# Backward pass of an S4 layer plus a gated FFN on one core: the stores of the decay exponentials go from ScalarE's DMA queue to SyncE's

## The chip, the cores and the metric

The kernel runs on one core of a Trainium2 chip. The time is device microseconds (us) of the whole program. The kernel before took 1819.65 us, the median of three runs (1815.38 to 1821.79).

## The reference, cut to what matters

A layer norm of `x` (2048 tokens, 576 channels) feeds an S4 convolution and a gated FFN; the reference returns the output and the gradients of everything in it but `B_x`.

```python
xn = _layernorm(x)
# A: S4
logdA = exp(log_dt)[:, None] * (A_re + 1j * A_im)          # 576 x 128
P = jnp.exp(logdA[:, :, None] * l[None, None, :])          # decay and phase at 2048 steps
K = jnp.einsum("dn,dnl,dn->dl", Cc, P, dB).real            # then y = causal convolution of xn with K by FFT
# B: FFN
gate = relu(xn @ W_gate); up = xn @ W_up                   # 576 -> 4608
out = x + (y + xn * Dskip) + (gate * up) @ W_down
_out, _vjp = jax.vjp(_f, ...); _grads = _vjp(grad_out)     # 13 outputs
```

## The kernel before, in words

**Two programs in one.** `Ffn.gen` and `S4.gen` are generators that emit instructions and yield an estimate of their TensorE time. The main loop runs `Ffn.gen` and, from the fourth layer-norm group on, lets `S4.gen` catch up to 0.9 of it (`PACE`). So TensorE carries FFN matmuls with small S4 matmuls strewn between them. The FFN loops over 12 chunks `c` of 384 hidden columns, and in each over 4 groups `sg` of 512 tokens:

- `a_unit` (L230): three products of 512 columns (gate, up, and the incoming gradient through `W_down`; L244), whose PSUM banks are read by ScalarE (`rg`, L252; `dhb`, L260) and VectorE (`upm`, L254), and then `hT`, `dgT`, `duT` on VectorE (L256 to L264).
- `t_steps` (L267): these three are turned by TensorE (L273) and copied into `hN`, `dgN`, `duN`.
- `outdx` (L277): the products back to 576 columns (L301), copied to `osx`, added up in DRAM by GpSimd's DMA queue (L312, L314).
- `dw_down`, `dw_gu`, `dw_left` (L330 to L378): the weight gradients of a chunk (L339, L355, L373), copied to `obd` and `obw` and stored by SyncE. They need the four token groups of the chunk, and run in the chunk after it. Their other operand, `rows`, is loaded by SyncE (L326) into four buffers.

All FFN products and turns take their PSUM banks from one rotation of five (`psum_mm`, L1146); S4 has three (`psum_s4`, L1147). `Balance.copy` (L56) gives each copy out of PSUM to VectorE (L62) or ScalarE (L68).

**S4 beside it.** In chunk 1, `S4.gen` runs `p1` (forward transforms of `xn` and the gradient: `fwd1`, L628 with stores of `A_ug`, L632; then `mix`, L645, which reads them back as `b_ug`, L707, writes `s_ug`, stores it, L722; `product`, L666 to L674, into `pr_z`; `unmix`, L655, into `fC`, stored at L728) and `params`, woven together by `both`. `params` holds what the change touches.

**The decay exponentials.** For each of 36 groups of 16 channels, `ex_step` (L582) takes a buffer `exs` of 128 x 640 fp32 from a pool of five (L568), multiplies on VectorE (L585), takes the exponential on ScalarE in place (L586), and stores 320 KB to `ex_dram` (L587). A buffer comes free when its store has landed, so `exs` number n+5 on VectorE waits for store number n. `p2` loads them again later (L817). In this text exs, Exp and store are numbered 1 to 36.

**What sets the order.** Every engine works its own list in order, and a DMA is issued by the engine in whose list it stands: an issue that waits holds up all behind it in that list. The lists are fixed when the program is built, and a scheduler moves instructions past one another there. SyncE (SP) does little else than issue transfers. The transfers of SP and ScalarE (ACT) share eight completion semaphores in turn: in the built lists each issue waits for the transfer that stands eight places before it.

Of the kernel before, what the change touches and what calls it, by code (L numbers as in the profile page):

```python
# [475 lines left out]
class S4:  # L476
# [85 lines left out]
    def params(self, pw):  # L562

        g, nc, bal = self.g, self.g.nc, self.g.bal
        v = nc.vector
        with ExitStack() as c:
            pool = self.pool(c, "par_raw", 1)
            exp_ = self.pool(c, "par_ex", 5)  # L568
            raw = pool.tile([P, 6, D], BF16, name="raw")
            nc.sync.dma_start(raw[:], self.par_in[:])  # L570
            ldt = pool.tile([P, D], BF16, name="ldt")
            nc.sync.dma_start(ldt[:], self.log_dt.rearrange("(o d) -> o d", o=1).to_broadcast([P, D]))
            yield 1.0
            dt = pool.tile([P, D], F32, name="dtf")
            nc.scalar.activation(dt[:], ldt[:], ACT.Exp)
            nc.sync.dma_start(self.dt_dram[:], dt[:])
            Ar, Ai, Br, Bi, Cr, Ci = (raw[:, i, :] for i in range(6))
            v.tensor_tensor(pw[:, 0, :], Ar, dt[:], op=ALU.mult)
            bal.add(d=0.7, a=0.7)
            yield 1.0  # L580

            def ex_step(i):  # L582
                shp = [P, SX, NE]
                ex = exp_.tile(shp, F32, name="exs")
                v.tensor_tensor(ex[:], pw[:, 0, i * SX:(i + 1) * SX].unsqueeze(2).to_broadcast(shp), self.ev[:].unsqueeze(1).to_broadcast(shp), op=ALU.mult)  # L585
                nc.scalar.activation(ex[:], ex[:], ACT.Exp)  # L586
                nc.scalar.dma_start(self.ex_dram[:, i], ex[:])  # L587
                bal.add(d=0.75, a=0.65)

            for i in range(0, 8):  # L590
                ex_step(i)
                yield 1.0
            p1 = pool.tile([P, D], F32, name="p1")
            p2 = pool.tile([P, D], F32, name="p2")
            v.scalar_tensor_tensor(pw[:, 1, :], Ai, 1.0 / TWO_PI, dt[:], op0=ALU.mult, op1=ALU.mult)
            for j, (y1, y2, op) in enumerate(((Br, Bi, ALU.subtract), (Bi, Br, ALU.add))):
                v.tensor_tensor(p1[:], Cr, y1, op=ALU.mult)
                v.tensor_tensor(p2[:], Ci, y2, op=ALU.mult)
                v.tensor_tensor(p1[:], p1[:], p2[:], op=op)
                v.tensor_tensor(pw[:, 2 + j, :], p1[:], dt[:], op=ALU.mult)  # L600
                bal.add(d=2.6)
                yield 2.0
            for i in range(8, D // SX):
                ex_step(i)
                yield 1.0
# [645 lines left out]
```

## Time and profile before

The profiled execution took 1815.38 us, the fastest of the three runs; its span, from the first to the last instruction, is 1813.7 us.

| | before |
|---|---|
| median of 3 runs | 1819.65 us |
| profiled execution, its span | 1815.38 us, 1813.7 us |
| busy: PE, DVE, ACT, POOL | 95%, 75%, 65%, 11% |
| mean granted TensorE clock | 0.993 |
| 36 `exs` multiplications (VectorE) | 825 ns each, started at 99.7 to 211.2 us |
| 36 Exp (ScalarE) | 737 ns each |
| 36 store issues (ScalarE's queue) | 326 ns each, at 102.1 to 231.7 us |
| store, issue to landing | 2.2 / 5.3 / 8.1 us (least, median, most) |

PE is TensorE, DVE VectorE, ACT ScalarE, POOL GpSimd, SP SyncE. "Idle before" an instruction is the time its engine waited, and the arrow names what ended the wait; `ACTq` and `SPq` rows are DMA issues. Durations of instructions that follow one another overlap a little, so starts are the better measure of pace (exs run back to back start 0.74 us apart, Exp 0.65 us).

### The profile page before, as it was taken

How to read it: one execution, taken by the hardware profiler on the slowest of the kernel's cores; microseconds unless marked ns; L12 is line 12 of the kernel's file. 1: busy time of each engine (PE TensorE's matmuls, PEld its weight loads, DVE VectorE, ACT ScalarE, POOL GpSimd, SP SyncE). 2: the span in 40 equal slices, each digit the busy share in tenths (PEclk: the TensorE clock that was granted, in tenths of full speed). 3: DMA queues.
4: the chain of work that ended last, by engine and by line, in shares of the span. 5: the costliest groups of instructions: out<-in, count | busy, mean ns of one | idle time of the engine just before them, and what ended most of it. 6: DMA issues, size and time to landing. Idle time of an engine off the chain costs nothing. (4 is left out here: it accounts for less than half of the span.)

```text
span 1813.7 us, 42172 instructions
## 1 busy us (share of the span) xinstructions
PE 1716.0 (95%) x16303; PEld 1184.1 (65%) x16449; DVE 1359.6 (75%) x3181; ACT 1182.3 (65%) x2710; POOL 205.2 (11%) x246
## 2 busy tenths in 40 slices
PE   7978998999999999999999999999899999999998
PEld 5655556668566666766756766766676775676776
DVE  7565886677889788679787889989979963983551
ACT  5865774687588478568468658748756845864551
POOL 0200012012012012011101101101111100110000
PEclk9989999999999999999999999999999999999999
DMA  9789899678558676777857856856666578995873
GB/s 300 264 313 339 267 246 291 181 194 229 179 130 208 176 193 133 223 196 154 219 159 179 233 165 141 218 180 152 170 175 150 94 213 276 256 279 153 265 244 96
DMA packets 239006, 373.32 MB, mean 206 GB/s; under 512 B 49490, under 2 KB 153428, under 8 KB 237268
## 3 DMA queue, kind: packets, MB, share of 16 engines
q1 hardware_dynamic: 207652, 292.29, 50.1%
q0 software_dynamic: 24384, 51.92, 18.9%
q10 hardware_dynamic: 6768, 26.40, 3.9%
q8 instruction: 129, 2.11, 0.5%
q14 instruction: 73, 0.60, 0.1%
HBM read 233.10 MB, written 137.43 MB: 204 GB/s over the span
## 5 line engine op out<-in xcount | busy, mean ns | idle before, releaser
L68 ACT CAST osx<-ps_mm 128x288 bf16<-128x288 f32 x675 | 255.4, 429 | 65.0 <-PE ps_mm L301 61.3
L314 POOL DMA_DIRECT2D acc_dram<-osx x160 | 138.7, 867 | 1058.8 <-ACT osx L68 645.3
L301 PE MATMUL ps_mm<-wf,dgT 128*128 128x288 bf16 x1152 | 207.2, 288 | 5.3 <-DVE upm L254 2.0
L355 PEld LDWEIGHTS <-rows 128*128 128x128 bf16 x1536 | 145.7, 98 | 94.7 <-issue 3.6
L301 PE MATMUL ps_mm<-wf,duT 128*128 128x288 bf16 x1152 | 207.2, 288 | 0.0
L301 PE MATMUL ps_mm<-wf,hT 128*128 128x288 bf16 x1152 | 183.3, 288 | 19.0 <-DVE hT L256 12.7
L244 PE MATMUL ps_mm<-xT,wd_156 128*128 128x512 bf16 x712 | 179.1, 379 | 0.4
L244 PE MATMUL ps_mm<-gT,wd_157 128*128 128x512 bf16 x693 | 175.7, 379 | 2.6 <-DMA gT<-in_gT_dram 2.0
L254 DVE SCALAR_TENSOR_TENSOR upm<-rg,ps_mm 128x512 bf16<-128x512 bf16 x144 | 98.5, 684 | 102.1 <-PE ps_mm L244 72.3
L244 PE MATMUL ps_mm<-xT,wd_155 128*128 128x512 bf16 x595 | 163.5, 379 | 11.3 <-ACT xT L153 1.6
L339 PE MATMUL ps_mm<-rows,hN 128*128 128x144 bf16 x2304 | 158.6, 226 | 0.0
L339 PEld LDWEIGHTS <-hN 128*128 128x128 bf16 x2304 | 147.5, 98 | 3.4 <-issue 0.8
L68 ACT CAST obw<-ps_mm 128x384 bf16<-128x384 f32 x104 | 49.5, 477 | 142.1 <-PE ps_mm L355 113.1
L301 PEld LDWEIGHTS <-hT 128*128 128x128 bf16 x1152 | 104.6, 98 | 50.6 <-DVE hT L256 16.9
L355 PE MATMUL ps_mm<-dgN,rows 128*128 128x384 bf16 x768 | 135.9, 326 | 1.0 <-ACT obw L68 1.0
L355 PE MATMUL ps_mm<-duN,rows 128*128 128x384 bf16 x768 | 136.6, 326 | 0.0
L301 PEld LDWEIGHTS <-duT 128*128 128x128 bf16 x1152 | 113.1, 98 | 31.1 <-issue 1.3
L301 PEld LDWEIGHTS <-dgT 128*128 128x128 bf16 x1152 | 107.7, 98 | 33.0 <-issue 8.0
L252 ACT ACTIVATE rg<-ps_mm 128x512 bf16<-128x512 f32 x144 | 87.2, 606 | 58.7 <-PE ps_mm L244 54.9
L932 DVE TENSOR_REDUCE Sm<-pr 128x8 f32<-128x256 f32 x288 | 120.0, 417 | 3.8
L68 ACT CAST dhb<-ps_mm 128x512 bf16<-128x512 f32 x141 | 83.8, 594 | 53.8 <-PE ps_mm L244 49.9
L244 PEld LDWEIGHTS <-wd_155 128*128 128x128 bf16 x720 | 66.2, 97 | 64.8 <-issue 6.2
(2517 smaller groups left out, 3517.5 us busy)
## 6 DMA issues: line engine op xcount, KB each, us to landing
acc_dram<-osx POOLq DMA_DIRECT2D x176, 288.0 KB, 4.9
gT<-in_gT_dram SPq DMA_DIRECT2D x48, 640.0 KB, 6.2
xT<-xT_dram SPq DMA_DIRECT2D x44, 640.0 KB, 6.2
rows<-in_gq_dram SPq DMA_DIRECT2D x48, 576.0 KB, 4.0
wf<-in_Wf_dram ACTq DMA_DIRECT2D x11, 1296.0 KB, 8.9
ex_dram<-exs ACTq DMA_DIRECT2D x36, 320.0 KB, 5.3
ex<-ex_dram SPq DMA_DIRECT2D x36, 320.0 KB, 4.1
out_dram<-obw SPq DMA_DIRECT2D x96, 96.0 KB, 2.8
```

The source lines that it names most:

```text
L68: self.nc.scalar.copy(out, in_)
L244: nc.tensor.matmul(ps[:], lhsT=w[:, k, fs], rhs=rhs[:, k, :], start=(k == 0), stop=(k == NK - 1))
L252: nc.scalar.activation(rg[:], ps_g[:], ACT.Relu)
L254: nc.vector.scalar_tensor_tensor(upm[:], rg[:], 0.0, ps_u[:], op0=ALU.is_gt, op1=ALU.mult)
L301: nc.tensor.matmul(ps[:, cs], lhsT=lt, rhs=rh, start=(i == 0), stop=(i == len(mms) - 1))
L314: nc.gpsimd.dma_start(g.acc_dram[:, t, :, :], o[:], accum_op=ALU.add)
L339: nc.tensor.matmul(ps[:, ft * 144:(ft + 1) * 144], lhsT=self.hN[:, st, ft * P:(ft + 1) * P], rhs=gq[:, st, :], start=(st == 0), stop=(st = ...
L355: nc.tensor.matmul(ps[:, :Fc], lhsT=xs[:, st, 0:P], rhs=src[:, st, :], start=(st == 0), stop=(st == ST - 1))
L932: nc.vector.tensor_reduce(out=Sm[:, vi, s0 + dd:s0 + dd + DG, :], in_=pr[:], op=ALU.add, axis=AX.X)
```

## The change

One line: the 36 stores are issued by SyncE.

```diff
@@ ex_step
                 nc.scalar.activation(ex[:], ex[:], ACT.Exp)
-                nc.scalar.dma_start(self.ex_dram[:, i], ex[:])
+                nc.sync.dma_start(self.ex_dram[:, i], ex[:])
                 bal.add(d=0.75, a=0.65)
```

The change has been described as "FFN products and FFN turns share one rotation of five PSUM banks instead of three and two"; both kernels have that rotation, and the diff holds nothing of it.

Because the scheduler places the instructions, the built lists differ in more than this line, from about the first exs to the first groups of `p2`; ahead of and behind that stretch they are the same. The number of instructions does not change. SP's list about the first stores, as built (before on the left):

```
L696 sig<-xn                          L696 sig<-xn
L697 sig<-grad_out                    L587 stores 1 to 6
L187 wd_157                           L697 sig<-grad_out
L187 wd_156                           L632 A_ug<-fA_1669
L632 A_ug<-fA_1669                    L587 store 7
L202 xT, L196 gT (token group 1)      L187 wd_157, wd_156
L611, L696, L697                      L632 A_ug<-fA_1699
```

And about the turn from `fwd1` to `mix`, where the old list has the same loads and no store of exs:

```
L632 A_ug (the last), L326 rows, L587 store 10
L707 b_ug x4, L345 obd, L326 rows, L360 obw
L587 stores 11, 12   L326 rows   L360 obw
L587 stores 13, 14   L360 obw
L587 stores 15, 16, 17   L360 obw
L587 stores 18 to 21   L722 s_ug   L707 b_ug   L360 obw   L587 store 22
```

On PE, seven transform matmuls (L628) stand ahead of the first L301 on the new `hT` of chunk 0's last group, where they stood 34 to 56 matmuls behind it. On DVE, one exs (the sixth) stands ahead of `upm` there, not behind it. On ACT, the first five Exp stand together with no issue between them.

## Prediction

> **What bounds the kernel now.** I first read the busy shares and the slices of the page, then busy time by stretch, then who waited for whom on PE, then the timelines of DVE, ACT and SP.
>
> ```profile
> PE 1716.0 (95%) x16303; PEld 1184.1 (65%) x16449; DVE 1359.6 (75%) x3181; ACT 1182.3 (65%) x2710; POOL 205.2 (11%) x246
> ...
> PE   7978998999999999999999999999899999999998
> ```
>
> PE is the bound: outside 98 us it works. So an edit can shorten the time only where PE stands still. Slices are 45.3 us; the third (digit 7) and fourth (8) hold the exs. By stretch (columns: length, PE, PEld, DVE, ACT, POOL busy, clock, DMA share, GB/s):
>
> ```profile
> 100.00:135.00 35.00, 22.99 (x219) 18.02 (x217) 23.89 (x44) 20.54 (x50) 2.31 (x5) 0.85 0.93 334
> 135.00:150.00 15.00, 14.95 (x153) 11.41 (x152) 5.09 (x10) 8.98 (x21) 0.00 (x0) 1.00 1.03 395
> 150.00:190.00 40.00, 34.04 (x220) 17.54 (x222) 25.45 (x54) 22.91 (x49) 0.00 (x0) 1.00 0.96 319
> 190.00:210.00 20.00, 17.25 (x141) 10.43 (x141) 16.94 (x48) 16.16 (x40) 1.75 (x2) 1.00 0.90 263
> 210.00:235.00 25.00, 24.20 (x187) 14.23 (x189) 19.80 (x57) 20.82 (x53) 3.38 (x4) 1.00 0.91 267
> ```
>
> PE idles 12.0 + 0.05 + 6.0 + 2.75 + 0.8 = 21.6 us there: all that the change can win or, so far as it makes such waits, add to. PE's waits from 90 to 240 us:
>
> ```profile
> PE ps_mm L301 <- DVE hT L256: 7.4, 1, 7.4
> PE ps_s_1748 L628 <- DVE fA_1669 L62: 2.7, 1, 2.7
> PE ps_mm L301 <- DVE upm L254: 2.6, 1, 2.6
> PE ps_s_2492 L645 <- ACT s_ug L68: 2.3, 1, 2.3
> PE ps_s_2520 L645 <- DVE s_ug L62: 1.9, 1, 1.9
> PE ps_s_1794 L628 <- DVE fA_1760 L62: 1.6, 1, 1.6
> ```
>
> The first two are one stall from 101.5 to 111.94. Why hT was late, DVE tells:
>
> ```profile
> 104.42 0.69 DVE L254 SCALAR_TENSOR_TENSOR upm<-rg,ps_mm 128x512 bf16<-128x512 bf16 x1
> 109.08 0.82 DVE L585 TENSOR_TENSOR exs<-pw,ev 128x640 f32<-128x640 f32 x1 [3.98 <-DMA ex_dram<-exs]
> 110.72 0.82 DVE L585 TENSOR_TENSOR exs<-pw,ev 128x640 f32<-128x640 f32 x1 [0.82 <-ACT exs L586]
> 111.47 0.42 DVE L256 TENSOR_TENSOR hT<-rg,upm 128x512 bf16<-128x512 bf16 x1
> ```
>
> The sixth and seventh exs stand ahead of hT and wait for buffers, that is for stores 1 and 2. These were issued at 102.14 and 102.8 on ACT and landed at about 109.05 and 110.7, by the exs that waited: 6.9 and 7.9 us, beside wd_157 and wd_156 (480 KB each, issued by SP at 101.83 and 102.36). The second cluster of stalls is at 160 to 170 us, and there ACT was held by its own issues:
>
> ```profile
> 159.62 1.77 ACTq L587 DMA_DIRECT2D ex_dram<-exs  x2
> 161.49 0.74 ACT L586 ACTIVATE exs<-exs 128x640 f32<-128x640 f32 x1 [5.84 <-DMA out_dram<-obw]
> 162.13 0.46 ACT L68 CAST obw<-ps_mm 128x384 bf16<-128x384 f32 x1
> ```
>
> An issue on ACT waited for an SP store (obw), as the eight shared semaphores demand, and the copies of obw and s_ug behind it freed PE's banks late.
>
> **Part 1, what is the same.** PSUM: line 1146 has the five banks already, 0 us. The number of bytes, exs and Exp is the same.
>
> **Part 2, issues from ACT to SP.** ACT loses 36 x 0.326 = 11.7 us of issues and its waits for semaphores (0.49, 3.24, 1.52, 1.34, 5.84 us: 12.4 in all). ACT is 65% busy, so that alone is worth nothing; it counts where PE waits, below. SP gets 36 x 0.33 = 12 us of issues in a stretch of 130 us where it had 92 issues to make. The price is that SP's loads stand behind stores that wait for their Exp.
>
> **Part 3, the stall at 101 us.** In the new list stores 1 to 6 go before the wd loads. DMA was nearly idle from 103.2 to 104.4 us (slices of 110, 23 and 58 GB/s), and A_ug, dt and sig, issued before them, are landing by then. Store 1 can be issued at 102.2. Its landing lies between 2.2 and 8.1 us, the least and most of the 36; I take 2.8, near the least, since nothing large is queued before it. It lands at 105.0, store 2 at about 105.8. Then DVE: exs 6 at 105.0, upm 105.8, exs 7 at 106.4, hT 107.2 to 107.6. On ACT five Exp without issues end near 104.9; the copies that the seven moved L628 need end near 107.8. PE goes on at 108.0 instead of 111.94: 3.9 us. The seven L628 (0.12 us each by starts) are done within the stall: 0.85. Of the 1.6 us wait at 119.88 for fA_1760, which now comes early, I count 0.25, as DVE is full from 113 to 127 us. Sum **5.0 us**. Between the ends: with 2.2, ACT's copies hold PE at 107.8 all the same (+0.2); with 8.1, hT comes at 112.7 and 0.75 of the 5.0 turns to nothing or a small loss.
>
> At half clock PE spent 112 to 115 us (granted 0.50 from 106 to 114, 0.82 to 116). It had fallen within 5 us of the gap's start (1.00 at 102 to 104, 0.62 at 104 to 106); the gap left is some 6 us, so I count nothing for the clock.
>
> **Part 4, 112 to 150 us.** PE is full, and the lead of 5 us is carried if operands are there: wd issued near 109.5, used 139; rows wait for PE's own release and move with it. 0 us.
>
> **Part 5, 146 to 174 us.** Here the new list is a chain. Store 11 stands on SP behind four b_ug loads, which wait for the last A_ug store (151.3 us before, 146.3 with the lead). Four b_ug issues (2.6 us, as before) and three more: store 11 issued 150.5. I call x its landing time and take 5.0: the median of the ACT stores in 150 to 190 us, where SP's own S_ug stores (288 KB) take 5.1:
>
> ```profile
> ex_dram<-exs ACTq DMA_DIRECT2D x16, 320.0 KB, 5.0
> b_ug<-A_ug_184 SPq DMA_DIRECT2D x8, 288.0 KB, 5.3
> ...
> S_ug_186<-s_ug SPq DMA_DIRECT2D x4, 288.0 KB, 5.1
> ```
>
> Landed 155.5; exs 16 (0.75), Exp 16 (0.7), then the third obw copy: 157.4. SP stores it and issues store 16 at 158.3; landed 163.3; exs 20 and 21 end 164.5, Exp 21 165.1, s_ug copy, PE's ps_2492 at 165.6 (before 166.44). Store 21 issued 165.2, landed 170.2; exs 26 ends near 171.9 behind what DVE does, pr_z 172.5, PE's L655 at 172.6 (before 174.4). The lead has shrunk from 5.0 to **1.7**. Three landings are in this chain: lead = 1.7 - 3 (x - 5.0), at most 5.
>
> A rule of the Trainium skill speaks against the change: DMA: Bandwidth & Descriptors, section "Queues, rings and completion order", says that each DMA engine goes round between the queue rows it has work for, so that on ACT's row a store shares the engines with SP's backlog, and on SP's row it stands behind it. By it x would grow. The rows above show no such advantage here (5.0 against 5.1). If the rule ruled, x would go toward the 8.1 of the most, and the sum below toward a loss of 4.7 instead of a gain of 4.6.
>
> **Part 6, 174 to 235 us.** Fewer exs stand on DVE between 177 and 190 us (none, where before there were four, one with a wait of 2.56), so dskip and upm come early and PE's 2.6 us wait at 198 goes: +2.6. Near 200 us exs 34 waits for store 29, which waits for an Exp late in ACT's list: DVE loses about 2 us, as it did before at 211 (2.04 us, after which PE waited 0.65); I count +0.3. The last store comes near 217, not 231.7; p2's loads keep their place.
>
> **Sum:** 1.7 + 2.6 + 0.3 = **4.6 us earlier**; 1815.38 becomes 1810.8. The median stands 4.3 us above the profiled run, so I give 1819.65 - 4.6 = **1815 us**. From p2's first groups on the lists are the same again, and what PE gains it keeps.
>
> **Rivals.** *A, slower:* stores land late on SP. The chain of part 5 decides: the gain is 4.6 - 3 (x - 5.0), nothing at x = 6.5, a loss of 4.7 at 8.1; if the 2.6 of part 6 are lost too, 7.3: 1824 to 1827. For it: SP's rows loads took 6.3 to 9.6 us and its A_ug stores up to 9.5 in 112 to 150 us, with DMA at 1.03. Against it: 5.1 from 150 on. *B, no change:* DMA is full from 130 to 170 us (share 0.92 to 1.04); the lead of part 3 then meets transfers that cannot come sooner, and 0 to 2 us remain: 1818. *C, more:* ACT is free of issues, so copies come sooner and x is 3.5 (the median of ACT's stores in 190 to 235 us); the lead stays 5, and 5 + 2.6 + 0.3 = 8 are won, 11 if half of the 6.0 us from 150 to 190 goes too: 1809 to 1812. *D:* that the diff doesn't do what it says is so for the PSUM words; it is in the sum as 0.
>
> **How the numbers follow.** Forecast (1 to 7 us faster) 0.36; A 0.28; B 0.20; C 0.16. A measurement can tell 0.3% (5.4 us) here. Faster by that: C, and a third of the forecast: 0.27. Slower: two thirds of A (0.19), and 0.06 for what no row shows: 0.25. Same: 0.48. The range goes from C's end, 1819.65 - 11, to A's end with a margin: **1808.5 to 1827.5**; the likeliest case alone has 1812.5 to 1818.5.
>
> **What would show it.** Part 3: stores 1 and 2 land within 4 us, hT at 107 to 108 us, PE idle 100 to 135 us near 7 instead of 12. Part 5: landing times of L587 between 145 and 170 (5 or 8), and PE's L655 (ps_2571) before or after 174.4. Part 6: no PE wait for upm near 198. Wrong if SP's loads (b_ug, xT, gT) come late behind a store and PE waits for a DMA, or if a new wait appears after 240 us.

## The result, and the profile after

The changed kernel takes 1807.84 us (median of four runs, 1805.36 to 1809.66) beside 1820.37 us of the kernel before (four runs): a ratio of 0.9935, with an interval of 0.9912 to 0.9958. A second measurement gave 0.9946 (0.9928 to 0.9964). The change is 10 to 12 us faster. The forecast had the side right, at 1815 us; the time lies just under the low end of its range (1808.5).

The profiled run of after took 1809.66 us, the slowest of its four, with a span of 1808.0; the profiled run of before was the fastest of its own. The two spans differ by only 5.7 us, so the difference has to be read stage by stage, not from the spans. The busy shares and PE's slices:

```profile
PE 1719.4 (95%) x16303; PEld 1185.2 (66%) x16449; DVE 1359.3 (75%) x3181; ACT 1181.1 (65%) x2710; POOL 205.0 (11%) x246
...
PE   7989989999999999999999999999999998999998
```

The work is the same. By stretch, with the columns as before:

```profile
100.00:135.00 35.00, 28.70 (x272) 22.16 (x271) 24.49 (x47) 24.75 (x61) 2.34 (x5) 0.90 1.01 366
135.00:150.00 15.00, 14.28 (x119) 9.66 (x120) 5.04 (x11) 5.23 (x11) 0.00 (x0) 1.00 0.94 303
150.00:190.00 40.00, 38.43 (x266) 20.25 (x268) 32.54 (x77) 28.23 (x67) 0.00 (x0) 1.00 0.89 311
190.00:210.00 20.00, 16.96 (x130) 10.23 (x131) 14.50 (x39) 15.78 (x39) 3.45 (x4) 1.00 1.04 304
210.00:235.00 25.00, 24.09 (x183) 14.47 (x184) 21.59 (x61) 21.44 (x54) 2.52 (x3) 1.00 1.03 330
```

PE now idles 6.3 us in the first stretch (12.0 before), 0.7 (0.05), 1.6 (6.0), 3.0 (2.75) and 0.9 (0.8): 12.5 in place of 21.6. What is left, from PE's waits from 90 to 240 us:

```profile
PE ps_s_2186 L628 <- DVE fA_2176 L62: 3.0, 1, 3.0
...
PE ps_mm L301 <- DVE upm L254: 1.7, 1, 1.7
```

The 7.4 us wait for hT is gone; a wait of 3.0 us is new. DVE's timeline shows both ends of this (the last number is the time that DVE stood before the row):

```profile
105.07 0.83 DVE L585 TENSOR_TENSOR exs<-pw,ev 128x640 f32<-128x640 f32 x1 [0.87 <-DMA ex_dram<-exs]
105.81 0.68 DVE L254 SCALAR_TENSOR_TENSOR upm<-rg,ps_mm 128x512 bf16<-128x512 bf16 x1
106.41 0.82 DVE L585 TENSOR_TENSOR exs<-pw,ev 128x640 f32<-128x640 f32 x1
107.14 0.42 DVE L256 TENSOR_TENSOR hT<-rg,upm 128x512 bf16<-128x512 bf16 x1
...
134.43 0.82 DVE L585 TENSOR_TENSOR exs<-pw,ev 128x640 f32<-128x640 f32 x1 [3.91 <-DMA ex_dram<-exs]
```

At 105 us the exs waits 0.87 us for store 1 where it waited 3.98. At 134.43 another exs waits 3.91 us, for store 9, and the copy that PE needs stands behind it. Store 9 was late because SP stood still; SP's waits from 120 to 136 us begin with

```profile
SPq L632 <- DMA wf<-in_Wf_dram: 5.0, 1, 5.0
```

The A_ug store ahead of store 9 shares its completion semaphore with `wf` (1296 KB, issued by ACT at 120.3 us), and has to wait until that has landed. The stores themselves, from 150 to 190 us (the last number is the median from issue to landing):

```profile
ex_dram<-exs SPq DMA_DIRECT2D x16, 320.0 KB, 3.1
S_ug_186<-s_ug SPq DMA_DIRECT2D x6, 288.0 KB, 3.6
```

They took 5.0 and 5.1 before. How far after is ahead of before, by the starts of the same instructions on PE:

| | before | after | lead |
|---|---|---|---|
| L301 on the new hT | 111.94 | 107.62 | 4.3 |
| first L339 | 127.64 | 120.21 | 7.4 |
| first L244 of chunk 1 | 144.32 | 140.27 | 4.1 |
| L655, ps_2571 | 174.09 | 165.93 | 8.2 |
| first L373 | 185.22 | 176.74 | 8.5 |
| L244 on the next token group | 188.76 | 180.06 | 8.7 |
| L339 of a later chunk | 1022.8 | 1014.8 | 8.0 |

So the time is won between 101 and 190 us and kept (0.3 us of each lead stands at 98 us already, ahead of anything that the change touches). Of the 8.0 us at 1015 us, 2.3 are missing from the difference of the spans: after, profiled in its slowest run, has two drops of the TensorE clock at 1516 and 1530 us that before, profiled in its fastest, hasn't.

### The profile page after: what moved, and what is told of

Same layout as the page of the kernel before. It is cut to its first block, busy times and chain, and to the rows that moved or that the text cites. A ratio compares the mean times of both kernels' runs of the same rounds, so it can differ in the third digit from the quotient of the medians.

```text
span 1808.0 us, 42163 instructions
## 1 busy us (share of the span) xinstructions
PE 1719.4 (95%) x16303; PEld 1185.2 (66%) x16449; DVE 1359.3 (75%) x3181; ACT 1181.1 (65%) x2710; POOL 205.0 (11%) x246
## 5 line engine op out<-in xcount | busy, mean ns | idle before, releaser
L301 PE MATMUL ps_mm<-wf,dgT 128*128 128x288 bf16 x1152 | 208.8, 289 | 4.7 <-DVE upm L254 2.0
L301 PE MATMUL ps_mm<-wf,duT 128*128 128x288 bf16 x1152 | 206.8, 289 | 0.0
L301 PE MATMUL ps_mm<-wf,hT 128*128 128x288 bf16 x1152 | 183.3, 288 | 10.0 <-DVE hT L256 4.9
L244 PE MATMUL ps_mm<-xT,wd_156 128*128 128x512 bf16 x712 | 179.1, 379 | 0.5 <-issue 0.2
L254 DVE SCALAR_TENSOR_TENSOR upm<-rg,ps_mm 128x512 bf16<-128x512 bf16 x144 | 98.5, 684 | 107.2 <-PE ps_mm L244 75.3
L244 PE MATMUL ps_mm<-gT,wd_157 128*128 128x512 bf16 x693 | 175.5, 379 | 1.9 <-DMA gT<-in_gT_dram 1.4
L244 PE MATMUL ps_mm<-xT,wd_155 128*128 128x512 bf16 x595 | 164.0, 379 | 10.8 <-ACT xT L153 1.7
L339 PE MATMUL ps_mm<-rows,hN 128*128 128x144 bf16 x2304 | 158.6, 226 | 0.0
L339 PEld LDWEIGHTS <-hN 128*128 128x128 bf16 x2304 | 147.4, 98 | 6.6 <-issue 3.9
L355 PE MATMUL ps_mm<-duN,rows 128*128 128x384 bf16 x768 | 136.6, 326 | 0.0
L301 PEld LDWEIGHTS <-duT 128*128 128x128 bf16 x1152 | 113.5, 99 | 30.4 <-issue 0.4
L301 PEld LDWEIGHTS <-hT 128*128 128x128 bf16 x1152 | 104.5, 98 | 39.3 <-issue 9.8
L301 PEld LDWEIGHTS <-dgT 128*128 128x128 bf16 x1152 | 108.3, 99 | 32.7 <-issue 7.2
L244 PEld LDWEIGHTS <-wd_155 128*128 128x128 bf16 x720 | 66.2, 97 | 64.3 <-issue 6.3
```

The costliest lines, as they stand in the source:

```text
L244: nc.tensor.matmul(ps[:], lhsT=w[:, k, fs], rhs=rhs[:, k, :], start=(k == 0), stop=(k == NK - 1))
L254: nc.vector.scalar_tensor_tensor(upm[:], rg[:], 0.0, ps_u[:], op0=ALU.is_gt, op1=ALU.mult)
L301: nc.tensor.matmul(ps[:, cs], lhsT=lt, rhs=rh, start=(i == 0), stop=(i == len(mms) - 1))
L339: nc.tensor.matmul(ps[:, ft * 144:(ft + 1) * 144], lhsT=self.hN[:, st, ft * P:(ft + 1) * P], rhs=gq[:, st, :], start=(st == 0), stop=(st = ...
L355: nc.tensor.matmul(ps[:, :Fc], lhsT=xs[:, st, 0:P], rhs=src[:, st, :], start=(st == 0), stop=(st == ST - 1))
```

## The experiments

**The theories.** *Theory 1:* the gain comes from when the stores land. An exs buffer is held until then, DVE stands at the exs that wants it, and copies that free PE's banks stand behind. *Theory 2:* the gain comes from ACT, which no longer issues and no longer waits there for other transfers' semaphores. *Theory 3:* it comes from the other order of the lists.

Ratios are those to the kernel before on the same chip. A table of all runs stands at the end of this section.

### Half of the stores each

```diff
# first8_sp                                    # last28_sp
-  nc.scalar.dma_start(self.ex_dram[:, i], ex[:])
+  (nc.sync if i < 8 else nc.scalar).dma_start(self.ex_dram[:, i], ex[:])      # first8_sp
+  (nc.scalar if i < 8 else nc.sync).dma_start(self.ex_dram[:, i], ex[:])      # last28_sp
```

> Stores 1 to 8 are issued by SP, stores 9 to 36 by ACT as before. Theory 1 (the gain comes from when the stores' transfers are made, so that buffers come free): PE goes on with L301 near 107.6 us as in the changed kernel (111.94 before) and its first L339 stands near 120.2 (127.64 before), and PE's idle time from 100 to 135 us is near 6.3 (12.0 before). From 150 us on it is like the kernel before, so it still loses some 6 us there: 6 to 8 us faster than before, ratio 0.9955 to 0.9967. Theory 2 (the gain comes from issues and semaphore waits that ACT no longer has): 8 of 36 issues leave ACT, 8/36 of 11.8 us is 2.6, ratio near 0.9986. Theory 3 (the gain lies in another order of the built lists, which only needs the first store to move): PE's lists from 112 us on differ from both, no number.

> Stores 1 to 8 are issued by ACT as before, stores 9 to 36 by SP. Theory 1: the stall at 101 us is as before (hT near 111.5, PE idle 12 us from 100 to 135), and from 150 to 190 us PE idles near 1.6 us as in the changed kernel instead of 6.0: 4 to 6 us faster, ratio 0.9967 to 0.9978. Theory 2: 28 of 36 issues leave ACT, 28/36 of 11.8 us is 9.2, ratio near 0.9950. If the two halves add up, this one and the run with the first eight on SP together give the 11.8 us of the whole.

Measured: 0.9980 (0.9966 to 0.9993) and 0.9996 (0.9980 to 1.0012). Together they give less than half of the whole; no theory had that. In the first, PE was where theory 1 wanted it (L301 at 107.8, first L339 at 120.5), and then lost all of it; its stretches:

```profile
100.00:135.00 35.00, 29.90 (x289) 23.19 (x288) 26.92 (x51) 24.36 (x63) 2.34 (x5) 0.90 1.02 368
150.00:190.00 40.00, 30.64 (x183) 14.80 (x182) 21.92 (x48) 20.21 (x45) 0.00 (x0) 0.87 0.84 276
```

PE idles 5.1 us in the first (12.0 before) and 9.4 in the second (6.0 before). DVE's and ACT's timelines show why:

```profile
157.17 0.83 DVE L585 TENSOR_TENSOR exs<-pw,ev 128x640 f32<-128x640 f32 x1 [6.03 <-DMA ex_dram<-exs]
```

```profile
157.96 0.48 ACT L68 CAST obw<-ps_mm 128x384 bf16<-128x384 f32 x1 [5.22 <-DMA out_dram<-obw]
```

DVE stands 6.0 us, and at 165.2 us 3.7 more, for stores that ACT issued, and ACT's obw copy waits 5.2 us until an obw store of SP has landed. PE waits 6.5 us for the s_ug copy behind the second of these exs. In `last28_sp` the stall at 101 us is as before, and a new one follows. DVE's timeline, and the landings of SP's stores from 112 to 150 us:

```profile
141.62 1.62 DVE L585 TENSOR_TENSOR exs<-pw,ev 128x640 f32<-128x640 f32 x2 [9.28 <-DMA ex_dram<-exs]
```

```profile
ex_dram<-exs SPq DMA_DIRECT2D x2, 320.0 KB, 9.6
```

Two stores issued at 132 us beside wf and rows land after 9.6 us; PE waits 5.3 us. Each half wins what it was to win and then meets a stall of the same kind elsewhere.

### Twenty-four of the stores

```diff
-  nc.scalar.dma_start(self.ex_dram[:, i], ex[:])
+  (nc.sync if i < 24 else nc.scalar).dma_start(self.ex_dram[:, i], ex[:])
```

> Stores 1 to 24 on SP, stores 25 to 36 on ACT. With the first eight alone on SP, PE was 7.1 us ahead of the kernel before at its first L339 and level with it again at its first L373 (185.7 against 185.2 us), after waits on ACT's stores between 150 and 166 us. If the stores of 110 to 175 us are what matters, this one keeps the changed kernel's lead there (first L373 near 177, against 185.2 before and 176.7 changed) and has its whole gain, ratio 0.993 to 0.996; the last twelve are worth under 2 us. If part 6 of the prediction (2.9 us from 174 us on) is right, it misses those 2.9 us: 0.996 to 0.997.

Measured: 0.9995 (0.9981 to 1.0009), outside what was expected. The lead is there at the first L373 (179.0 us: 6.2 ahead), and the last twelve stores lose it. DVE's timeline:

```profile
234.53 0.83 DVE L840 TENSOR_TENSOR xa<-pw,ev 128x640 f32<-128x640 f32 x1 [5.00 <-DMA ex_dram<-exs]
```

The last store is issued on ACT at 227.2 us (208.1 in the changed kernel), and `p2`'s first large multiplication, which waits for it, holds DVE for 5.0 us with upm behind, for which PE then waits 2.3 us at 236.5. PE idles 3.5 us from 190 to 210 and 3.4 from 235 to 260 (0.9 before). The same kernel shows both queues side by side, in its landings from 150 to 190 us:

```profile
ex_dram<-exs SPq DMA_DIRECT2D x14, 320.0 KB, 3.1
ex_dram<-exs ACTq DMA_DIRECT2D x6, 320.0 KB, 5.4
```

### More buffers

```diff
-  exp_ = self.pool(c, "par_ex", 5)
+  exp_ = self.pool(c, "par_ex", 8)
```

> The kernel before with a pool of eight exs buffers instead of five; all stores stay on ACT. Theory 1: no exs waits for a store at 105 to 111 us, so upm and hT come as soon as their inputs, hT near 107, PE's L301 goes on near 107.5 instead of 111.94 and the exs later wait less on DVE (27.6 us in 12 waits before, under 10 here): 4 to 8 us faster, ratio 0.9956 to 0.9978. Theory 2: ACT has all its issues and its waits for shared semaphores, so at most 2 us faster, ratio 0.9989 to 1.0010.

> The changed kernel with eight exs buffers. Theory 1 (what costs is DVE standing at an exs whose buffer a store still holds, with copies behind it that PE needs): the 3.9 us wait of exs on DVE before 134.4 and PE's 3.0 us after it are gone, DVE waits for exs stores under 4 us in all (11.8 in the changed kernel), and it is 2 to 4 us faster than the changed kernel, some 0.002 lower in its ratio. Theory 2 (ACT's issues and semaphore waits are what costs): beside the run of before with eight buffers (0.9965) it gains 8 to 12 us from ACT's freedom alone, ratio 0.990 to 0.992. If the two are one cost that either edit takes away, the ratio stands within 0.001 of the changed kernel's.

Measured: 0.9965 (0.9951 to 0.9978) for the kernel before with eight buffers, 0.9941 (0.9923 to 0.9960) for the changed one. With every store on ACT, the buffers alone bring L301 to 107.8 and half of the gain. That is theory 1, and this much needs no freedom of ACT. PE idles 7.8 us from 100 to 135 us there, in place of 12.0.

On the changed kernel the buffers gain nothing that the intervals can tell from its 0.9946. The 3.0 us stall at 132.7 is gone as expected, but DVE's waits for stores went up to 17.4 us in 5 (11.8 in 7), against theory 1's "under 4": the lists put more exs ahead, and a later one waits longer. So the sum of DVE's waits for stores is no measure of the loss; what counts is what PE needs behind them.

### The wf load on another queue

```diff
-                self.load_wf(c)
+                self.load_wf(c, g.nc.gpsimd if c == 1 else None)
```

> The changed kernel with the second wf load (1296 KB, for the second slice of d_ff) issued by GpSimd instead of ACT, so that no transfer on SP waits for wf through a shared semaphore. If that wait (5.0 us of SP at 125 to 130 us, which makes store 9 late, the exs wait 3.9 us on DVE and PE wait 3.0 us at 132.7 to 135.7) is a cost of its own, these three waits go and the kernel is 3 us faster than the changed one: ratio to the kernel before 0.9918 instead of 0.9935. If the store is late for another reason (DMA full at that time), the wait stays and the ratio is 0.993 to 0.994; if wf lands later on GpSimd's queue and PE waits for it at the first L301 of the next slice, it is slower than that.

> The changed kernel with eight exs buffers and the second wf load on GpSimd's queue. With five buffers the wf edit took away the 3.0 us stall at 132.7 us, and a new one of 4.1 us (s_ug on ACT) came at 160 to 170 us. If that new stall is again a store that holds a buffer, eight buffers take it away, PE idles under 13 us from 100 to 300 us (18.3 in the changed kernel), and the ratio is 0.990 to 0.992. If it comes from a copy behind a late transfer of another kind, the ratio is that of the eight buffers alone.

Measured: 0.9950 (0.9933 to 0.9967), and with eight buffers as well 0.9954 (0.9938 to 0.9969). The 3.0 us wait went in the first, so the shared semaphore was its cause (SP has no wait for wf there), but PE then waits 4.1 us for s_ug at 162.7 us, and the time is the same. In the second that wait is gone, and one of 4.2 us stands at 135 to 150 us instead. Neither beats the changed kernel.

### All stores on GpSimd's queue

```diff
-  nc.scalar.dma_start(self.ex_dram[:, i], ex[:])
+  nc.gpsimd.dma_start(self.ex_dram[:, i], ex[:])
```

> All 36 stores on GpSimd's queue, five exs buffers: neither ACT nor SP issues them, and no shared semaphore ties them to SP's transfers. Theory 1: what counts is when a store lands; the first two are issued at 102 to 103 us ahead of the wd loads, so L301 goes on near 107.6 to 108 as in the changed kernel, and later stalls depend on landings; with landings of 3.5 to 6 us as acc_dram has on that queue, 0.993 to 0.997. Theory 2: ACT is as free as in the changed kernel and SP freer, so the ratio is at or under the changed kernel's, and stalls like the 3.0 us at 132.7 (a store held on SP behind a wait for wf) are gone.

Measured: 1.0051 (1.0035 to 1.0067), 9 us slower than before. ACT has no issue of a store and no wait for SP's semaphores here, so ACT's freedom alone does not give the gain. DVE's timeline at the first stall, and the landings of the first six stores from 96 to 112 us:

```profile
109.05 0.82 DVE L585 TENSOR_TENSOR exs<-pw,ev 128x640 f32<-128x640 f32 x1 [4.67 <-DMA ex_dram<-exs]
```

```profile
ex_dram<-exs POOLq DMA_DIRECT2D x6, 320.0 KB, 8.3
```

The first stores are issued from 101.66 us, no later than in the changed kernel, and land after 8.3 us instead of 3.5.

### Small extra transfers

```diff
                 nc.sync.dma_start(self.ex_dram[:, i], ex[:])
+                nc.scalar.dma_start(self.dum_dram[:, i], self.ev[:])    # aft_actdum
+                nc.sync.dma_start(self.dum_dram[:, i], self.ev[:])      # aft_spdum
```

> The changed kernel, with a second, small DMA (20 KB, the row of exponents to a scratch tensor that nobody reads) issued by ACT behind each Exp; the stores themselves stay on SP. No exs buffer waits for it. Theory 2 (ACT's issues and its waits on shared semaphores are what the stores cost before): ACT has 36 issues and such waits again, and most of the 10 us is lost, ratio 0.998 to 1.000. Theory 1 (late landings hold exs buffers): it loses only what 36 issues of 0.33 us and some late copies cost PE, under 3 us, ratio 0.994 to 0.9965; SP's own DMAs also wait on these small ones through the shared semaphores, which land sooner than the stores.

> The control of the run with small DMAs on ACT: the same 36 small DMAs (20 KB, the row of exponents to a scratch tensor), issued by SP instead of ACT; the stores are on SP as in the changed kernel. Theory 2 (an issue on ACT stands in ACT's order and keeps its copies and Exps waiting for other transfers): ACT is free here, SP has 36 issues more, and the kernel keeps most of the changed kernel's gain, ratio 0.994 to 0.9965. If the loss of that run came from 36 more transfers and semaphore turns, or from any shift of the order that puts a store beside wf and rows, this one loses it too, ratio 0.998 to 1.001.

Measured: 0.9996 (0.9982 to 1.0010) on ACT and 1.0009 (0.9994 to 1.0025) on SP. The first alone would have spoken for theory 2. Its control loses as much with ACT free of these issues, so the loss need not be their price; that both kernels lose for one reason is not shown. (Nothing ties these small transfers to an Exp, and the scheduler put some of them ahead of the exs.) With the transfers on ACT, an exs at 136.6 us waits 7.26 us for a store, and PE 3.6 us for a copy behind it; ACT itself waits 5.4 us, in three waits before copies at 149 to 155 us, for the small transfers. With them on SP, SP's longest wait for a transfer from 90 to 240 us, DVE's timeline and the stretch around it (L699 and L586 of this kernel are L697 and L585 of the others):

```profile
SPq L699 <- DMA wf<-in_Wf_dram: 6.1, 1, 6.1
```

```profile
144.67 0.83 DVE L586 TENSOR_TENSOR exs<-pw,ev 128x640 f32<-128x640 f32 x1 [8.75 <-DMA ex_dram<-exs]
```

```profile
135.00:150.00 15.00, 14.91 (x118) 9.72 (x117) 4.73 (x9) 3.90 (x8) 0.00 (x0) 1.00 0.96 327
```

More transfers turn the eight semaphores differently, another one meets wf, and a store further down SP's list holds DVE 8.75 us. But PE idles only 0.1 us in that stretch: this wait costs nothing by itself. The loss comes later: an exs at 158.58 us waits 8.78 us for a store, ACT's obw copy 6.46 us for an obw store, and PE idles 9.0 us from 150 to 190 us.

### The burst of exs spread

```diff
             for i in range(0, 8):
                 ex_step(i)
-                yield 1.0
+                yield 3.0
```

> The changed kernel with the first eight exs steps spread: a cost of 3.0 instead of 1.0 between two of them for the planner, so that DVE's list has two exs in a row at 100 us instead of five. What is left of the stall at 101 us in the changed kernel (PE idles 6.3 us from 100 to 135 us) comes from the five exs that stand on DVE ahead of copies and upm. If that is so, PE idles under 3 us there, the drop of the clock after it (3.4 us lost) goes, and it is 4 to 7 us faster than the changed kernel: ratio 0.9905 to 0.993. If the steps only move to where they hold up something else, the ratio is 0.9935 to 0.997.

Measured: 1.0045 (1.0031 to 1.0058). The stall at 101 us did nearly go (L301 at 104.8, 7.1 us ahead of before), but the exs moved behind it wait 27.8 us for stores, PE waits 7.4 us for a copy behind one of them and idles 9.8 us from 100 to 135 us, and the lists after 300 us differ as well. It is the rival that was named, and worse: beside the second profile of the changed kernel PE idles 9.9 us longer from 100 to 300 us (25.8 beside 15.9) and 6.2 us longer from 300 us on (55.8 beside 49.5). No run looks into that second part.

### The changed kernel again, and all runs

> The changed kernel once more, with more rounds beside the kernel before on one chip. Over the runs so far the span falls by 1.4 us for each 0.001 of mean granted clock (33 spans of the kernel before: 0.986 to 0.995), and the four runs of the changed kernel had a mean of 0.9938, the 33 of before 0.9894. If the changed kernel's higher clock is its own (fewer gaps after which the clock falls), the ratio stays at 0.9935; if half of the gain was the luck of four runs, the ratio is 0.9960 to 0.9968, which is the 6 to 7 us that are left at equal clock.

Measured: 0.9946 (0.9928 to 0.9964), between the two cases, with an interval that takes in both; the mean clock (0.986 to 0.992 in the 33 runs of before: the 0.995 in the expectation is that of runs of other kernels) was again higher than that of before (0.9930 beside 0.9902). Span times clock, the time at full clock, is 1799.4 us for 33 runs of before and 1794.7 and 1794.9 for the two measurements of after. By this measure some 5 us of the gain are there at equal clock, and the rest is that the clock falls less. But the measure counts a drop of the clock as lost time even while PE stands idle. In the two profiles that is so for 3.7 of the 5.1 us of before's first drop and for 0.7 of the 3.4 us of after's, so some 3 us that it gives to the clock belong to the stall at 101 us.

PE's idle time from 100 to 300 us, and the time lost to a lower clock there (one minus the granted clock, summed over the time), from each profiled run:

| | ratio | PE idle | clock lost | longest wait of DVE for a store |
|---|---|---|---|---|
| before | 1 | 27.6 | 6.8 | 4.0 |
| first 8 on SP | 0.9980 | 22.0 | 10.3 | 6.0 |
| first 24 on SP | 0.9995 | 22.0 | 8.6 | 4.2 |
| last 28 on SP | 0.9996 | 26.6 | 13.6 | 9.3 |
| before, 8 buffers | 0.9965 | 18.6 | 8.5 | 3.3 |
| after | 0.9935 | 18.3 | 5.1 | 3.9 |
| after, again | 0.9946 | 15.9 | 6.8 | 3.2 |
| after, 8 buffers | 0.9941 | 15.0 | 5.1 | 5.7 |
| after, wf on GpSimd | 0.9950 | 17.1 | 8.5 | 6.5 |
| after, both of these | 0.9954 | 15.8 | 8.5 | 5.6 |
| after, 36 small on ACT | 0.9996 | 19.9 | 10.2 | 7.3 |
| after, 36 small on SP | 1.0009 | 24.5 | 10.2 | 8.8 |
| after, burst spread | 1.0045 | 25.8 | 9.0 | 7.7 |
| stores on GpSimd | 1.0051 | 30.3 | 18.8 | 6.7 |

(In the profiles of before, after and the 36 small on SP 146 of 16449 matmul records are missing, so their idle time reads a little too long.)

The sum of the two middle columns ranks the kernels nearly as the ratios do: 20 to 26 for all that keep the gain, 30 to 49 for all that don't, 27 for the one that has half of it. The mean spans of the 14 rows follow that sum with a correlation of 0.91. Half-clock time in which PE stands idle is in both columns; PE's idle time alone ranks the kernels as well (15.0 to 18.3, 19.9 to 30.3, and 18.6; 0.92). So the loss and the gain go with PE's stalls in this stretch (a part of the spread burst's loss lies behind it); DVE's waits for stores don't give it. Not all of these stalls come from stores of exs: before's idle time has 3.4 us in it, near 280 us, and after's 3.5, in which PE waits for loads of `bC` (L684).

## Why the prediction was right, and where its sizes were off

**The side was right, by the steps named.** The stall at 101 us was released as described: exs 6, upm, exs 7 and hT were predicted at 105.0, 105.8, 106.4 and 107.2, and began at 105.07, 105.81, 106.41 and 107.14. Eight buffers on the kernel before released it too (L301 at 107.8), without the change: it was the buffer that held it. The size, 4.6 us forecast beside some 8.5 by the same instructions and 10 to 12 by the medians, was that of rival C, which had 8 to 11. Term by term:

- **Part 2, ACT's freedom as worth nothing by itself:** not refuted. Stores on GpSimd's queue give ACT the same freedom and lose 9 us; small transfers on ACT cost no more than the same on SP. A price of ACT's issues by themselves isn't shown, and isn't excluded where they stand before a copy that PE needs, as in the kernel before at 161 us (5.84 us). The 5.2 us wait with the first eight on SP is no such case: there the wait ended with an obw store, for which the copy itself waited, as it does for 6.46 us in the run with the small transfers on SP, where ACT issues none of them.
- **Part 3, 5.0 us at the first L339:** 7.4. L301 came 4.3 us earlier (3.9 was predicted; 0.3 were there before). From it to the first L339, PE's stretches in before and in after are:

```profile
111.94:127.64 15.70, 13.78 (x103) 10.29 (x104) 13.88 (x27) 10.07 (x29) 1.77 (x4) 0.91 0.88 317
107.62:120.21 12.59, 12.48 (x97) 9.59 (x97) 11.63 (x24) 8.62 (x23) 1.78 (x4) 0.89 1.02 343
```

  The mis-sized term is the wait for fA_1760 and what stands beside it: PE idled 1.9 us there and now 0.1, so 1.8 were won where 0.25 was counted. The rest is PE's busy time, 1.3 us shorter, chiefly by the seven L628 that are done within the stall (0.85 was counted). The clock was rightly counted at nothing: behind L301 it costs 1.4 us in both.
- **Part 4, nothing at 112 to 150 us:** a loss of 3.3. "SP's loads stand behind stores that wait" was seen as the price; that a store stands behind an A_ug store, which waits on wf's semaphore, was not. A new wait was looked for after 240 us; it came at 132.7.
- **Part 5, a lead of 1.7 at L655:** 8.2. Two terms failed. One is the chain's start: the last A_ug stores landed at 142.1 us (151.6 before; 146.3 was taken), so store 11 was issued at 147.2, not at 150.5. The other is x, the landing on SP: a median of 3.1 where 5.0 was taken from ACT's row. Of the three landings of the chain, the first took 4.7 us, as counted, and stores 16 and 21 2.7 and 2.8. The formula gives 1.7 + 3 x 1.9 = 7.4 with the median, which is luck, as it leaves out the start; and its 1.7 counts from 174.4, where ps_2571 began at 174.09. That it cannot exceed the 5.0 of part 3 was wrong as well, since before's own 6.0 us of idle time from 150 to 190 us fell to 1.6. The step from "S_ug on SP takes 5.1 today" to "stores there will take 5.0" held the other transfers fixed, and they moved: S_ug too went from 5.1 to 3.6 (and to 3.4 with the first eight on SP, where the stores of this stretch are on ACT, so the stores' queue alone isn't what moves it).
- **Part 6, 2.9 us after 174 us:** nothing more. The upm wait at 198 only fell from 2.6 to 1.7, and PE's idle time from 190 to 235 rose from 3.55 to 3.95: stores land in 5.6 us there, where they took 3.5 before. (In the second profile of the changed kernel that idle time is 2.6, so up to 0.9 may be won.)

**The rivals.** A (late landings on SP) needed x over 6.5 and had 3.1. But late landings on SP do occur: 9.6 us in `last28_sp`, with a PE wait of 5.3 us behind them, and DVE's waits of 8.8 us in `aft_spdum`, each with wf or rows beside the store, and neither kernel kept the gain. B (transfers that cannot come sooner) is refuted by the lead. The rule that spoke against the change (the Trainium skill, DMA: Bandwidth & Descriptors, "Queues, rings and completion order") would have x grow on SP's row. In this stretch it shrank in every kernel: medians of 2.6 to 3.8 from 150 to 190 us in ten profiles with stores on SP, 5.0 to 5.8 in four with stores on ACT, among them the one kernel that has both. From 190 to 235 us it is the other way about (3.5 on ACT in before, 5.6 on SP in after). The measurement decides; why SP's row is quicker from 150 to 190 us no run tells.

**What stays open.** Theory 1 explains the stall at 101 us, the new one at 132.7 us and those in which DVE stands at an exs ahead of PE's copy; eight buffers alone give half of the gain. For the other half it is argued from the profiles, stall by stall. Why the changed list meets few such stalls, and most lists tried beside it more, is a matter of order and timing (theory 3); no run holds the order fixed while the queue changes. The drops of the clock that an average run of before has and its profiled, fastest run has not (a mean clock of 0.989 beside 0.993) were not seen, so the part of the gain that is the clock's rests on the means of the runs alone. In the profiled pair the drops from 100 to 300 us took 2.9 us from PE's work in before and 4.1 in after.

## What to carry to other kernels

A store from a small pool of buffers is a wait for the engine that fills the next buffer: ask for each such store what it stands behind on its issuing engine, and whose completion semaphore it or its neighbour shares (here a load of 1296 KB that stands eight transfers earlier). Half a change can be worth nothing where the parts hide each other: the first eight stores alone won 7 us by 120 us and had lost them by 186 us. Before crediting a mechanism after one run that "adds the cost back", run the control that adds it elsewhere; here the control lost as much.

## What the runs showed of the hardware

**The clock falls in fixed portions.** In the 14 profiles, every drop of the granted clock that ends within the span lasts 3.4 us at half clock or a multiple of it (6.8, 10.2, 13.7), which is 1.7 us of clock for each 3.4. After's stretches near 720 us, where PE waits once, 1.9 us for hT, and the clock falls 0.6 us later (the first number behind the length is PE's busy time, the clock is the third from the end):

```profile
718.78:720.72 1.94, 0.00 (x1) 0.01 (x1) 1.94 (x6) 0.84 (x3) 0.00 (x0) 1.00 0.91 210
721.34:724.75 3.41, 3.41 (x28) 2.38 (x26) 3.41 (x9) 2.25 (x6) 0.00 (x0) 0.50 1.03 402
```

A wait of 1.9 us cost 1.7 more, while the wait of 3.0 us at 132.7 in the same run cost none. The Trainium skill (TensorE: Matmul & The Clock Gate, "Why this matters for your kernels") asks for no idle gaps over about 3 us between bursts; the portion agrees with the window of about 3.4 us of its Part 1, but a wait well under the bound was followed by a drop here. What a drop costs is only its part on working PE. The first drops of before and after, with PE's busy time:

```profile
104.49:114.73 10.24, 2.81 (x18) 2.09 (x18) 4.79 (x10) 3.99 (x9) 0.00 (x0) 0.50 0.99 391
103.53:110.36 6.83, 5.42 (x24) 2.77 (x24) 5.33 (x12) 5.38 (x14) 0.00 (x0) 0.50 0.99 360
```

Before's drop is longer, but 7.4 us of it fall on idle PE, so it took half of 2.8 us, 1.4, from its work, and after's 2.7. A stall is priced at its length plus none, one or more portions of 1.7 us, as far as they outlast it.

**Run to run, the clock is most of the spread.** Over 33 runs of before, spans from 1813.9 to 1825.8 us go with mean clocks from 0.992 to 0.986, some 1.4 us for each 0.001 (correlation -0.81); span times clock varies by 1.9 us (standard deviation), the spans by 3.1.
